# Selective attention and a low-rank mixer on one core: the first two batches are fed in another order

## The chip, the cores and the metric

One core of a Trainium2 chip runs the whole kernel as one program. The metric is device time in microseconds; the median of three runs before the change is 416.16 (416.15 to 417.01).

The engines: TensorE (PE; PEld is its weight load), VectorE (DVE), ScalarE (ACT), GpSimd (POOL) and SyncE (SP). Each runs its own instructions in order. "SPq", "ACTq" and "POOLq" are those engines' queues in which they issue DMAs; a DMA that waits there holds all that is behind it.

## The reference, cut to what matters

Eight batches, eight heads, 576 positions, head size 64. Attention with a causal mask and a bias from running sums of a gate s, then a mixer over 576 positions of width 512.

```python
scores = (q @ k.T) / sqrt(D)
cum    = cumsum(maximum(s, 0))
scores = where(causal, -1e9, scores + minimum(-(cum[:, None] - cum[None, :]), 0))
x      = softmax(scores) @ v            # heads side by side: 576 x 512
u = x + (x.T @ U @ V).T                 # rank 32
out = u + maximum(u @ w_ch1, 0) @ w_ch2 # 512 -> 2048 -> 512
```

Inputs and output are float32; the kernel computes in bfloat16 with float32 sums.

## The kernel before, in words

**Tiling.** The batches go in four groups of two (`GROUPS`). A group has 1152 rows, nine tiles of 128; tile 4 (`TAIL`) holds the last 64 rows of both batches. For a group: attention of both batches fills `x_sb`, `mix` (batch 0 alone: `mix_first`) turns it into `uT`, `layer1` gives `hT` and `layer2` the output, which goes out by SP (L508, L513).

**Scores.** q and k lie in `qT` and `kT` with the head size on the partitions, two heads (a pair n) to a buffer, in a ring of eight. Four more partitions, D to KA, hold the bias as products: rows of `parts` (a running sum split into bfloat16 pieces, and its negative) against rows of ones. So a score with its bias is one matmul over 68 rows (L280). `scores` computes a head in four PSUM banks, ACT takes the exponential of each (L286), POOL zeroes the upper triangle of five diagonal blocks (L299), and `weigh` multiplies by v (L326) and normalises on DVE (L332, L334, L339). Batch 0 has eight probability tiles of its own (`first_p`), three of them lent from `x_sb[1]` and `v_raw[1]`; later heads rotate over five.

**How q and k come in.** For batches 0 and 1: `load_six` (POOL's queue, with a cast) into a corner of `hT`, then `turn_six`: six PE transposes (L260) and two copies (L272). Batch 1 does its eight turns inside `attention(1)`, two ahead of head 0 and one in each of heads 0 to 5. For batches 2 to 7: `cast(b)` (L144, POOL's queue) writes bfloat16 copies to DRAM (`kq_rows`), and `turn_kq(n)` (L163, SP's queue) reads a pair back with a transposing DMA; `bias_rows(n)` (L251, SP) then overwrites partitions D to KA from `aug_rows` in DRAM, so it waits for that pair's transposes. The 64 elements behind each pair in `kq_rows` are zeros that the transposed read runs into.

**The sums.** `cumulate(b0, b1)` is a generator in steps: gate and scans (L212, L214), a small matmul that adds the sums of earlier segments (L217), then additions and splits into `parts` (L219 to L226), all on DVE. For batches 0 and 1 `direct_rows` (L231) writes `parts` straight into `qA` and `kA`. For batches 2 to 7 `later_sums` runs `cumulate(2, B)`, clears `ones` and `zeros` on POOL, sends them to `aug_rows` and `kq_rows` (L633, L634), and `keep_rows` (L238) sends `parts` to `aug_rows`. It is called after batch 1 and ahead of the turned loads of batch 2; its tiles are lent from `x_sb[1]`.

**v.** `fetch_v(b, t)` (L176) brings a tile as float32 into `vf`; `cast_v` (L182, POOL) copies it into `v_raw`. One `vf` serves all batches, so a batch's loads wait for the casts of the one before. Batch 0 is fetched on ACT's queue at the very start.

**Order around the change.** It is written out by hand (`manual_schedule`). `first_attention` is batch 0: three turns, then scores of eight heads with the other turns in between; two heads are weighed after head 6, six at the end, with `mix_first` in two halves. `beside(back, ahead, ratio, lead)` interleaves two generators by their estimated PE time: `layer1` of batch 0 beside `attention(1)` and `mix(0)`, then the layers of group g beside the attention of group g + 1. `at_head(h)` hangs work on other queues on a head: weight loads, casts of q and k, casts of v. SP's order after batch 1 is:

```python
    for n in range(8, 16):
        if n == 12:
            for t in range(5):
                fetch_v(3, t)
        turn_kq(n)
        if n > 8:
            bias_rows(n - 1)
```

From batch 2 on, every second head queues `bias_rows(n + 7)` and `turn_kq(n + 8)`, and head 7 of batch c the loads of v of batch c + 2. The casts of v of batch c + 1 stand in POOL's queue at heads 5 to 7 of batch c, ahead of the next head's mask.

The lines are those of the kernel before:

Of the kernel before, what the change touches and what calls it, by code (L numbers as in the profile page):

```python
# [40 lines left out]
def kernel(  # L41
# [34 lines left out]
    v_raw = [const([128, 10, H, D + 1], BF16, f"v_raw{i}") for i in range(2)]  # L76
# [23 lines left out]
    def clear(ap, value=0.0, engine=None):  # L100
# [11 lines left out]
    lent = x_sb[1].rearrange("p t c -> p (t c)")  # L112
    run_all, cum_all = (
        lent[: SEG * H, many * i : many * i + many].bitcast(FP32) for i in range(2)
    )
    ones, zeros = lent[:BH, 2 * many : 2 * many + S], lent[:BH, 2 * many + S : 2 * many + S + D]
# [25 lines left out]
    def cast(b):  # L142
        for i, src in enumerate((k, q)):
            nc.gpsimd.dma_start(  # L144
                out=kq[i, HP * b : HP * b + HP, :PAIR].rearrange("n (r c) -> r n c", r=128),
                in_=src[b]
                .rearrange("(n h) s d -> n (h s d)", h=2)
                .rearrange("n (r c) -> r n c", r=128),
            )
# [53 lines left out]
    def cumulate(b0, b1):  # L203
# [19 lines left out]
        nc.vector.tensor_sub(rest, cum, pt[:, 1])  # L223
        nc.vector.tensor_copy(pt[:, 2], rest)
        yield
        nc.vector.tensor_sub(pt[:, 3], rest, pt[:, 2])  # L226
# [49 lines left out]
    def scores(n, hh, p):  # L276
# [11 lines left out]
        ps = bank("s", 3)  # L288
        one(ps, 0, S - 128, 512, 64)
# [14 lines left out]
        ps = bank("s", 3)  # L304
        one(ps, 0, 0, 128, 448)
# [38 lines left out]
    spare = v_raw[1].rearrange("p t h e -> p (t h e)")  # L344
    first_p = pT + [lent[:, :P_W], lent[:, P_W : 2 * P_W], spare[:, :P_W]]
# [187 lines left out]
    for t in (4, 0, 1, 2, 3):  # L533
        fetch_v(0, t, nc.scalar)
    load_six(0, 0, 0, 2)
    nc.vector.memset(before, 1.0)
    nc.vector.memset(warm, 0.0)
    nc.scalar.activation(warm, warm, EXP)
    before_v = before.rearrange("p (h j) -> p h j", j=SEG)
# [8 lines left out]
    load_six(0, 1, 0, 2)  # L548
# [4 lines left out]

    for t in (kT[0], qT[0]):
        clear(t[D:KA, : 2 * S], 1.0)
    sums = cumulate(0, 2)
# [3 lines left out]
    for i in range(2, HP):  # L560
        for t in (kT[i], qT[i]):
            clear(t[D:KA, : 2 * S], 1.0, nc.gpsimd)
    next(sums)
# [7 lines left out]
    for r in range(AUG):  # L571
        direct_rows(0, 1, HP, r)
    load_UV()
    load_s(2, B)

    for p in first_p:
        nc.gpsimd.memset(p[:, PAD:D4], 1.0)

    def first_attention():
        turn_six(0, 0, 0)  # L580
        turn_six(0, 0, 1, scalar=2)
# [3 lines left out]
        for h in range(H):  # L585
            p = next_p()
            quanta = scores(h // 2, h % 2, p)
# [13 lines left out]
            if h == 2:  # L601
                cast_v(0, 4)
                load_w1(0)
                load_w1(1)
                cast_v(0, 2)
                cast_v(0, 3)
                cast_v(0, 0, nc.vector)
                cast_v(0, 1, nc.vector)
            if h == 3:
                place_UV(0)  # L610
                for t in range(5):
                    fetch_v(1, t)
            if 3 < h < 6:
                clear((kA, qA)[h - 4][1][D:KA], 1.0, nc.gpsimd)
# [11 lines left out]
        for _ in mix_first(2):  # L626
            pass

    def later_sums():
        yield from cumulate(2, B)  # L630
        clear(ones, 1.0, nc.gpsimd)
        clear(zeros, 0.0, nc.gpsimd)
# [123 lines left out]
```

## Time and profile before

| what | value |
|---|---|
| median of 3 runs | 416.16 us |
| profiled execution, its time | 419.31 us |
| its span | 417.5 us |
| PE busy | 377.2 us, 90% |
| PEld, DVE, ACT, POOL busy | 235.8, 146.3, 202.1, 105.2 us |
| share of the chain that ended last | PE 81%, DVE 5%, DMA 4%, POOL 3% |
| DMA: SP's queue (q1), POOL's (q0), ACT's (q10) | 38.4%, 20.7%, 1.5% of 16 engines' span |
| moved | 48.55 MB, mean 116 GB/s |

The profile is of one execution. "busy" is the time in which an engine ran an instruction; "idle before, releaser" is the time an instruction's engine stood still and what ended it. In rows of the order of time, the first number is the start and the second the length of a merged run of instructions, both in us; a row of a queue covers the issue and not the transfer. PEclk is the granted share of TensorE's clock. A DMA share over 1 means that transfers overlap on an engine.

### The profile page before, as it was taken

The numbers are of one execution on the slowest core, as the hardware profiler recorded it, in microseconds if no ns is written. First come the engines' busy times: TensorE is split into PE (matmuls) and PEld (weight loads), VectorE is DVE, ScalarE is ACT, GpSimd is POOL, SyncE is SP. The second block draws the span as 40 slices with busy tenths as digits, with TensorE's granted clock in tenths as the row PEclk, the third lists the DMA queues.
The fourth block names the chain that finished last, engine by engine and source line by source line (L and its number), as shares of the span: only waits on it lengthen the run. The fifth ranks groups of instructions, "written<-read, shape, count | busy, mean of one in ns | idle before, by whom it ended". The sixth has DMA issues, their size and how long they took to land.

```text
span 417.5 us, 8214 instructions
## 1 busy us (share of the span) xinstructions
PE 377.2 (90%) x3255; PEld 235.8 (56%) x3278; DVE 146.3 (35%) x317; ACT 202.1 (48%) x472; POOL 105.2 (25%) x170
## 2 busy tenths in 40 slices
PE   2698799999689819999999999999999999999996
PEld 1576686547467514566665545666665455665442
DVE  6657584812113304811113348111123373000221
ACT  2581486308658600098896400688875002775000
POOL 7498267003234121032332300123222000000000
PEclk9999699999969968999999999999999999999999
DMA  9599999499989896998896991100001111000121
GB/s 164 100 169 178 194 183 202 91 155 172 203 152 215 145 173 122 200 201 184 176 189 106 192 215 52 54 0 2 2 2 52 51 52 75 2 0 2 75 77 75
DMA packets 117943, 48.55 MB, mean 116 GB/s; under 512 B 99536, under 2 KB 113040, under 8 KB 117904
## 3 DMA queue, kind: packets, MB, share of 16 engines
q1 hardware_dynamic: 99424, 33.21, 38.4%
q0 software_dynamic: 13792, 13.63, 20.7%
q10 hardware_dynamic: 4688, 1.18, 1.5%
q8 instruction: 26, 0.43, 0.4%
q14 instruction: 13, 0.11, 0.1%
HBM read 37.52 MB, written 16.97 MB: 131 GB/s over the span
## 4 chain that ended last, share of the span: by engine, by line
PE 81%; DVE 5%; DMA 4%; POOL 3%; ACT 2%; issue 2%; SPq 1%; ACTq 0%; POOLq 0%; DVEq 0%
PE ps_f L481 29%; PE ps_f L496 28%; PE ps_s L280 10%; PE ps_pv L326 8%; PE ps_f L423 2%; PE ps_pv L441 2%; PE ps_f L456 1%; ACT pT L286 1%; SPq L163 1%; DMA kT<-parts 1%; POOL pT L299 1%; ACT hT L488 1%; DVE x_sb L460 1%; DMA qT<-kq_rows 1%; DMA vf<-in_v_dram 1%
## 5 line engine op out<-in xcount | busy, mean ns | idle before, releaser
L481 PE MATMUL ps_f<-uT,w 128*128 128x384 bf16 (+1 forms) x832 | 161.2, 318 | 0.3 <-ACT hT L488 0.3
L286 ACT ACTIVATE pT<-ps_s 128x448 bf16<-128x448 f32 x244 | 115.4, 517 | 91.9 <-PE ps_s L280 90.5
L496 PE MATMUL ps_f<-w,hT 128*128 128x512 bf16 x554 | 139.9, 381 | 1.4 <-issue 0.2
L488 ACT ACTIVATE hT<-ps_f 128x384 bf16<-128x384 f32 (+1 forms) x208 | 99.1, 477 | 71.8 <-PE ps_f L481 70.5
L280 PE MATMUL ps_s<-qT,kT 68*128 68x128 bf16 (+4 forms) x576 | 87.1, 258 | 13.0 <-DMA qT<-aug_rows 5.7
L299 POOL TENSOR_SCALAR_AFFINE_SELECT pT<-pT 128x640 bf16<-128x640 bf16 x61 | 45.8, 751 | 200.8 <-ACT pT L286 200.5
L481 PEld LDWEIGHTS <-w 128*128 128x128 bf16 x832 | 74.1, 99 | 34.9 <-issue 1.5
L496 PEld LDWEIGHTS <-hT 128*128 128x128 bf16 x576 | 53.3, 98 | 55.3 <-issue 2.7
L280 PEld LDWEIGHTS <-kT 68*128 68x128 bf16 x576 | 49.9, 104 | 43.2 <-issue 15.9
L332 DVE RECIPROCAL rec<-ps_pv 128x5 f32<-128x5 f32 x64 | 12.5, 195 | 146.9 <-PE ps_pv L326 146.4
L505 DVE TENSOR_TENSOR o<-x_sb,ps_f 128x512 f32<-128x512 bf16 x36 | 24.7, 686 | 91.6 <-PE ps_f L496 81.5
L326 PE MATMUL ps_pv<-v_raw,pT 128*128 128x65 bf16 x915 | 41.9, 201 | 10.7 <-POOL pT L299 9.6
L326 PEld LDWEIGHTS <-pT 128*128 128x128 bf16 x915 | 38.6, 102 | 19.4 <-POOL pT L299 10.4
L334 DVE TENSOR_TENSOR x_sb<-ps_pv,rec 128x320 bf16<-128x320 f32 (+1 forms) x64 | 29.3, 458 | 2.5 <-ACT pT L286 0.4
L182 POOL CAST v_raw<-vf 128x512 bf16<-128x512 f32 (+1 forms) x38 | 22.9, 618 | 14.6 <-DMA vf<-in_v_dram 14.0
L460 DVE TENSOR_TENSOR x_sb<-x_sb,ps_f 128x512 bf16<-128x512 bf16 x32 | 21.2, 686 | 5.3 <-PE ps_f L456 5.1
L448 DVE COPY uT<-ps_pv 128x1024 bf16<-128x1024 bf16 (+2 forms) x18 | 11.1, 624 | 2.6 <-PE ps_pv L441 2.4
L272 DVE COPY kT<-ps_pv 64x576 bf16<-64x576 bf16 x12 | 9.6, 799 | 4.3 <-PE ps_pv L260 4.2
L441 PEld LDWEIGHTS <-x_sb 128*128 128x128 bf16 x128 | 8.7, 98 | 3.8
L456 PE MATMUL ps_f<-ux_sb,V_cat 128*128 128x512 bf16 x27 | 10.2, 379 | 0.6 <-DVE o L505 0.4
L260 PEld LDWEIGHTS <-hT 96*128 96x128 bf16 x96 | 7.3, 125 | 5.2 <-DMA hT<-in_q_dram 2.7
L441 PE MATMUL ps_pv<-identity,x_sb 128*128 128x128 bf16 x128 | 10.2, 219 | 0.0
(88 smaller groups left out, 131.8 us busy)
## 6 DMA issues: line engine op xcount, KB each, us to landing
out_dram<-o SPq DMA_DIRECT2D x32, 256.0 KB
vf<-in_v_dram SPq DMA_DIRECT2D x28, 256.0 KB
w<-in_moe_w_ch_dram POOLq DMA_DIRECT2D x8, 512.0 KB, 8.7
kq_rows<-in_k_dram POOLq DMA_DIRECT2D x6, 576.0 KB, 7.9
kq_rows<-in_q_dram POOLq DMA_DIRECT2D x6, 576.0 KB, 10.5
vf<-in_v_dram ACTq DMA_DIRECT2D x4, 256.0 KB
out_dram<-o SPq DMA_DIRECT2D x8, 128.0 KB
vf<-in_v_dram SPq DMA_DIRECT2D x7, 128.0 KB
```

Source lines behind the costliest of these rows:

```text
L182: (engine or nc.gpsimd).tensor_copy(v_raw[b // 2 % 2][n, 5 * (b % 2) + t, :, :D], vf[n, t])
L280: nc.tensor.matmul(ps[:, col : col + w], lhsT=kt_[:KA, c + kc : c + kc + 128], rhs=qt_[:KA, c + qc : c + qc + w], start=True, stop=True,)
L286: nc.scalar.activation(p[:, at : at + w], ps[:, :w], EXP, scale=scale)
L299: nc.gpsimd.affine_select(out=diagonal, in_=diagonal, compare_op=ALU.is_ge, fill=0.0, base=0, pattern=[[0, 5], [1, 128]], channel_multipli ...
L326: nc.tensor.matmul(pv3[:, it, :], lhsT=p[:, at : at + 128], rhs=vr[:, 5 * bi + j, h, :], start=(j == 0), stop=(j == it),)
L334: nc.vector.tensor_mul(x[:, 5 * bi : 5 * bi + n, h * D : h * D + D], pv3[:, :n, :D], rec[:, :n].unsqueeze(2).to_broadcast([128, n, D]),)
L441: nc.tensor.transpose(pb[:, d, m, :], x[:, t, 128 * d : 128 * d + 128], identity)
L460: nc.vector.tensor_add(x[:, t, :], x[:, t, :], hp_)
L481: nc.tensor.matmul(f1[:, :cw], lhsT=w1[:, kt, 128 * nf : 128 * nf + 128], rhs=uT[:, kt, c0:c1], start=(kt == 0), stop=(kt == 3),)
L488: nc.scalar.activation(hT[:, nf, c0:c1], f1[:, :cw], RELU)
L496: nc.tensor.matmul(f2, lhsT=hT[:, kt, 128 * t : 128 * t + 128], rhs=w2[:, kt, :], start=(kt == 0), stop=(kt == 15 and not more),)
L505: nc.vector.tensor_add(o, x_sb[g % 2][:, t, :], f2)
```

## The change

- The tiles of the later sums, `ones` and `zeros` are lent from `v_raw[1]` instead of `x_sb[1]`. `ones` and `zeros` are cleared and sent in head 2 of batch 0. `cumulate(2, B)` is taken apart: scans in head 3 of batch 0 (DVE), the small matmul, its addition (DVE) and a copy and a product (now POOL) in head 4, two more steps on POOL in heads 0 and 1 of batch 1, `keep_rows` in head 3 of batch 1. `later_sums` is gone.
- v of batch 0 is fetched on SP's queue behind the bias rows of batch 0, not on ACT's at the start; its casts are all on POOL in head 3 (two were on DVE). s of the later batches comes ahead of U and V.
- The rows of ones of batch 1 come from `aug_rows` by two DMAs; two POOL clears of `kA[1]` and `qA[1]` are gone. The bias rows of batch 1 and the first half of its q and k are queued in `first_attention`.
- The first two turns of batch 1 move into the second half of `mix_first`; the other six follow two heads earlier.
- `cast` writes runs of 2304 elements instead of 576.
- Products of zeros on PE (`fill`): five of 512 columns before the first sums, six before the third turn, two of 384 in each head of batch 0. The matrix is the first tile of `x_sb[0]`, and the scores overwrite what they write.
- The second load of batch 0 is issued ahead of two masks on POOL; `scalar=2` (copies on ACT) moves from the second turn to the first; the place of `place_UV` shifts by one head.

```diff
-    lent = x_sb[1].rearrange("p t c -> p (t c)")
+    lent = [x_sb[1].rearrange("p t c -> p (t c)"), v_flat[1]]
...
-                out=kq[i, HP * b : HP * b + HP, :PAIR].rearrange("n (r c) -> r n c", r=128),
+                out=kq[i, HP * b : HP * b + HP, :PAIR].rearrange("n (r c) -> r n c", r=32),
...
-    def cumulate(b0, b1):
+    def cumulate(b0, b1, engine=nc.vector):
...
+        nc.vector.tensor_add(cum, run, ps[:n, :nb].unsqueeze(2).to_broadcast([n, nb, CW]))
         yield
-        nc.vector.tensor_add(cum, run, ps[:n, :nb].unsqueeze(2).to_broadcast([n, nb, CW]))
-        nc.vector.tensor_copy(pt[:, 1], cum)
-        nc.vector.tensor_scalar_mul(pt[:, 0], pt[:, 1], -1.0)
+        engine.tensor_copy(pt[:, 1], cum)
+        engine.tensor_scalar_mul(pt[:, 0], pt[:, 1], -1.0)
...
+    def fill(ps, w):
+        nc.tensor.matmul(ps[:, :w], lhsT=zero[:, :128], rhs=zero[:, :w], start=True, stop=True)
...
-        turns = [(hp, which) for hp in range(HP) for which in range(2)] if b == 1 else []
+        turns = [(hp, which) for hp in range(HP) for which in range(2)][2:] if b == 1 else []
...
-    for t in (4, 0, 1, 2, 3):
-        fetch_v(0, t, nc.scalar)
...
+    zero = x_sb[0][:, 0, :]
+    clear(zero)
...
+    for t in (4, 0, 1, 2, 3):
+        fetch_v(0, t)
+    load_s(2, B)
     load_UV()
-    load_s(2, B)
+    later = cumulate(2, B, nc.gpsimd)
...
-            quanta = scores(h // 2, h % 2, p)
+            quanta = scores(h // 2, h % 2, p, fills=384)
...
             if h == 2:
+                clear(ones, 1.0, nc.gpsimd)
+                clear(zeros, 0.0, nc.gpsimd)
+                nc.sync.dma_start(out=kq[:, :, PAIR:].rearrange("i n c -> (i n) c"), in_=zeros)
+                nc.sync.dma_start(
+                    out=aug[1:4].rearrange("r n s -> n r s"),
+                    in_=ones.unsqueeze(1).to_broadcast([BH, 3, S]),
+                )
+            if h == 3:
                 cast_v(0, 4)
                 load_w1(0)
                 load_w1(1)
...
+                next(later)
+            if h == 4:
+                place_UV(0)
+                next(later)
+                next(later)
             done.append((0, h, p))
             if h == 6:
+                load_six(1, 0, 0, 4)
+                load_six(1, 1, 0, 4)
...
+        nc.sync.dma_start(out=kA[1][D : D + 1], in_=aug_v[3:4, HP : 2 * HP])
+        nc.sync.dma_start(out=qA[1][D + 1 : KA], in_=aug_v[1:4, HP : 2 * HP])
+        for r in range(AUG):
+            direct_rows(1, 0, HP, r)
...
-        for _ in mix_first(2):
+        half = mix_first(2)
+        next(half)
+        turn_six(1, 0, 0)
+        turn_six(1, 0, 1)
+        for _ in half:
             pass
-    def later_sums():
...
     def at_head(h):
-        if h == 2:
+        if h < 2:
+            next(later)
+        if h == 3:
             place_UV(1)
+            keep_rows(2, B)
...
-    for _ in later_sums():
-        pass
```

More of the change, by code (lines that the diff above doesn't have):

```diff
@@ L111 @@
     many = 2 * (B - 2) * CW
[L112 removed]
+    lent = [x_sb[1].rearrange("p t c -> p (t c)"), v_flat[1]]
     run_all, cum_all = (
[L114 to L116 removed]
+        lent[1][: SEG * H, P_W + many * i : P_W + many * i + many].bitcast(FP32)
+        for i in range(2)
+    )
+    at = P_W + 2 * many
+    ones, zeros = lent[1][:BH, at : at + S], lent[1][:BH, at + S : at + S + D]
     U_f = stage[:, : 5 * R].rearrange("p (t r) -> p t r", r=R)
@@ L555 @@
         clear(t[D:KA, : 2 * S], 1.0)
+    ps = bank("s", 3)
+    for _ in range(5):
+        fill(ps, 512)
     sums = cumulate(0, 2)
```

67 lines of the change are left out of this document (27 added, 40 removed).

## The prediction

> **What bounds the kernel now.** I read the slices of the page first, then the stages around the weak slices, then the order of time of TensorE, of SyncE's queue and of GpSimd in those stages, then the DMA issues. Slices of 10.4 us:
>
> ```profile
> PE   2698799999689819999999999999999999999996
> ...
> PEclk9999699999969968999999999999999999999999
> DMA  9599999499989896998896991100001111000121
> ```
>
> TensorE (PE) is full from slice 15 to the end. It is weak at the start, in slice 10, and in slices 13 and 14, and after each of those holes its granted clock is low too. The DMA engines are busy for the first 250 us, with one hole in slice 7. The stages (columns: PE, PEld, DVE, ACT, POOL busy, clock, DMA share, GB/s):
>
> ```profile
> 110.00:118.00 8.00, 2.28 (x17) 1.59 (x15) 0.19 (x1) 2.17 (x7) 1.22 (x2) 0.83 0.96 189
> ...
> 140.00:154.00 14.00, 5.13 (x53) 2.92 (x50) 1.82 (x6) 3.80 (x9) 1.52 (x3) 0.84 0.72 147
> 154.00:176.00 22.00, 20.45 (x135) 10.93 (x138) 13.12 (x24) 0.93 (x2) 3.64 (x6) 0.87 0.84 160
> 176.00:264.00 88.00, 87.28 (x775) 53.17 (x780) 28.96 (x65) 48.44 (x112) 20.49 (x30) 1.00 0.84 163
> ```
>
> From 176 on PE has nothing to lose. The two holes, in the order of time of PE and of GpSimd (POOL):
>
> ```profile
> 116.44 0.53 PE L280 MATMUL ps_s<-qT,kT 68*128 68x64 bf16 x4 [5.72 <-DMA qT<-aug_rows]
> ...
> 154.59 1.01 PE L326 MATMUL ps_pv<-v_raw,pT 128*128 128x65 bf16 x15 [9.41 <-POOL pT L299]
> ...
> 153.23 0.61 POOL L182 CAST v_raw<-vf 128x512 bf16<-128x512 f32 x1 [12.18 <-DMA vf<-in_v_dram]
> ```
>
> The first hole waits for the bias rows of the last head pair of batch 2. In the second, POOL sits in a cast of v of batch 4 whose load has not landed, and the masking behind it holds PE. Both loads stand in SyncE's (SP's) queue, which runs in order:
>
> ```profile
> 71.59 0.56 SPq L633 DMA_DIRECT2D kq_rows<-x_sb  x1
> ...
> 81.56 1.84 SPq L238 DMA_DIRECT2D aug_rows<-parts  x4
> 83.58 1.32 SPq L163 DMA_TRANSPOSE kT<-kq_rows  x1
> 84.99 1.53 SPq L163 DMA_TRANSPOSE qT<-kq_rows  x1
> ...
> 98.55 11.32 SPq L176 DMA_DIRECT2D vf<-in_v_dram  x5
> ...
> 113.77 0.28 SPq L251 DMA_DIRECT2D qT<-aug_rows  x1
> ...
> 149.74 4.20 SPq L176 DMA_DIRECT2D vf<-in_v_dram  x5
> ```
>
> The queue stands still until 71.59 behind POOL's two clears (`ones`, `zeros`), then until 81.56 for the sums on DVE, and only then begins the turned loads of batch 2. From 83.58 to 149.74 it is late all the way. So the time is set by when SP begins at L163, plus 66.2 us of its own work to the load of v of batch 4, plus what PE has left after 154.59. That is the number to move.
>
> **The later sums, ones rows and zeros (the part that decides).** All that the queue waited for at 71.59 and 81.56 goes away: ones and zeros are written in head 2 of batch 0, the scans go in head 3, the rest on POOL by head 1 of batch 1, and the four `keep_rows` are queued in head 3 (before: about 56 us). What ends last for the first turned load is then the cast of k of batch 2 into DRAM. In the DMA issues it is sent at 59.97 and takes 9.4 us: 69.4. The q cast, sent at 60.71, takes 13.2: 73.9. The casts of batch 3 land at 76.1 and 79.7 (62.88 + 13.2, 63.60 + 16.1). So SP's start moves from 83.58 to somewhere between 69.4 (14.2 us gained) and 79.7 (3.9, if the transposes get nothing beside the casts). I take the second transfer, 84.99 to 73.9, as the step that holds the rest in order: 11.1.
>
> Then the contention. Five v loads take 7.74 us (24.31) and 7.86 (36.79) where they share little, and 11.32 at 98.55 beside the two casts of batch 4: a pair of casts costs the queue about 3.5 us. In the new order the first transposes stand beside the casts of batch 3 (3.5 lost), the v loads come ahead of the casts of batch 4 (3.5 won back), and the transposes after them take those casts instead (3.5 lost): 11.1 - 3.5 = 7.6 by that count, 11.1 if transposes, which SP issues only every 1.3 to 1.5 us, lose less than v loads do. I take 10 and keep 7.6 to 11.1.
>
> The first hole closes within this: bias rows land at 116.3 - 10 = 106.3 and PE stands for them from 110.7. That gives 5.72, and the slow stretch behind it: granted clock 0.67 in 114 to 118 and 0.50 in 118 to 122, so about 2.7 of the time to 121.8. The PE that comes 8.4 us earlier then meets the second hole sooner: it would stop at 145.2 - 8.4 = 136.8 and go on at 154.6 - 10 = 144.6. The second hole stays, at 7.8 us, with its slow stretch. This is where the gain ends, and why it is 10 and not the 20 of both holes.
>
> **POOL's new work.** Copy, multiply, subtract, copy, subtract over 72x384, four of them beside or between the masks of 0.75 us. On DVE they took 0.36, 0.22, 0.55, 0.36 and 0.56. POOL's nearest rows are casts of 0.62 for 128x512. Bounds: 2.0 us (as on DVE) to 4 (twice). In batch 1 the masks come every 3 us with 2 us idle ahead of them (2.28, 2.39), so 0.9 to 1.8 in head 0 beside a weight load's issue of 0.77 just fits: 0, and at worst 0.5 once. Two clears of 2.01 leave POOL and two casts of 0.6 come to it from DVE: it is lighter.
>
> The Trainium skill (GPSIMD Engine Reference, Elementwise side by side) has a two-input operation about 1.96 times slower on GpSimd than on VectorE. No run here shows it; by it the two subtractions would be about 1.1 us each, an estimate, inside those bounds.
>
> **v of batch 0 on SP behind the rows.** Five issues leave ScalarE's queue (5.37 us) and five come to SP, ahead of s and U, V. Before, the first scores waited for rows sent at 8.05 that landed at 13.39, 5.3 us, while v held 45% of the DMA engines in 0 to 7 us and 41% in 7 to 14. A small transfer on idle engines took 1.85 (s, at 0.81). First scores at 10.2 to 13.4; I take 11: 2.5 won. v then is sent from about 12 to 18 and lands by about 20; POOL wants it in head 3, near 20. Cover: the scores of three heads. If gone, POOL's weight loads, v of batch 1 and everything behind wait for it.
>
> **Products of zeros.** Cold, 512 columns take 0.43 (the pairs of L496 in 155 to 157 are 0.85), warm 0.22. Eleven of 512 and sixteen of 384 are 9.9 us cold, 5 warm. The eleven lie in PE's idle time before the first scores (11.3 us idle of 14). The sixteen lie beside the exponentials, which take 1.7 us a head while PE has 1.4 cold and 0.7 warm for the scores; two products more are 0.64 or 0.32. The first three heads also have transposes and run 2.5 us a head, bound by PE. So the products cost up to 3 x 0.64 + 5 x 0.3 = 3.4 if PE stays cold, and win up to 3 x 0.8 = 2.4 if it is warm; later weighs then run at 0.46 instead of 0.83. Two new waits of PE lie here: its matmul of the later sums in head 4 waits for DVE's scans (1.6 us, queued behind the last copy of turns), about 1.5; and the products of head 7 read `x_sb`, which DVE has just written: rec and product, 0.7. What is queued behind each is the next head's scores, and ScalarE waits for them.
>
> **Turns ahead.** Four copies of 0.8 us move ahead of the uT copies: layer 1 begins up to 3.2 later, but the scores no longer wait 2.82 for them (43.99). Even. Then the second half of q and k of batch 1 is wanted in head 0 instead of head 2, near 45; it lands at 39.14 + 9.5 = 48.6. A stall of up to 3.6 if the start came early, 0 otherwise.
>
> Together the start lies between 6 us earlier and 4 later, and none of it reaches the end: PE has 7.8 us of waiting left at the second hole, and the casts queue behind weight loads that keep the DMA engines full from 64 to 70 (share 121.8%, 208 GB/s). I count 0.
>
> **Longer runs in casts.** That same row bounds it: one queue alone already fills the engines. 0; at best, a tenth of four casts' 2.8 us of transfer each, 1 us. The Trainium skill (DMA: Bandwidth & Descriptors, Specifications) asks 512 B for line rate, and both forms are above it: it also gives 0.
>
> **Sum.** The profiled execution took 419.31 with a span of 417.5; the median is 416.16. 417.5 - 10 = 407.5 of span, and against the median 416.2 - 10 = 406.
>
> **Rivals.**
> 1. The second hole goes too. For: between 141 and 149 the DMA share is low, so the queue there waits link by link (transpose landed, then bias, then the next), and if it comes before the casts of batch 5 instead of beside them the links shorten. PE then loses neither hole: 5.7 + 2.7 + 9.4 + 2.5 (cold to 159.6) + 0.6 at 78 to 80 = 20.9, time 395. Against: it needs 18 us, more than 14.2. Chance 0.20.
> 2. Casts starve the transposes. In 100 to 102 the cast queue had 108.6% of the engines and SP's queue 0.0%, with one packet. Then the start is 79.7, 3.9 gained: 412. Chance 0.15. By the Trainium skill (DMA: Bandwidth & Descriptors, Queues, rings and completion order) an engine takes turns between queues packet by packet, a packet being many descriptors; longer runs would make the casts' turns longer, and that row agrees.
> 3. Slower: v of batch 0 lands so late that POOL stands in its cast in head 3, with both weight loads, v of batch 1, the halves of q and k and the casts of batch 2 behind it. It turns slower where the casts come over 14.2 us late, v landing after 34. For: SP's v loads have taken 11.3 us and three transfers are behind it. Against: two such stretches end at 12 + 11.3 + 3.4 = 27. At 38 it would be 4 slower, 420. Chance 0.06.
> 4. It changes nothing at the end, because some other wait in front of 83.58 (a lane of earlier transfers) keeps SP: 416. Chance 0.03.
>
> **How the numbers follow.** Forecast 0.54 (gain 7 to 13, 403 to 409), rivals 0.20, 0.15, 0.06, 0.03, and 0.02 for more than rival 1. Likeliest: 406. The range reaches to both neighbours, 394 to 412, and leaves out rivals 3 and 4, the last, and the outer part of rival 1: under 0.2. Faster by over 0.2% (0.8 us, what a measurement here can tell): 0.54 + 0.20 + 0.15 + 0.02, less 0.01 for a weak rival 2: 0.90. Within: 0.03 and that 0.01; slower 0.06.
>
> **What would show it.** Right: L163 begins at 70 to 75 on SP; no wait of PE for aug_rows near 105; a POOL wait for vf of about 8 us near 137, ended near 143; PE over 95% behind it. Wrong: L163 at 79 or later; the wait for vf gone or over 11 us; a POOL wait for vf near 20; PE slow through batch 0.

## The result and the profile after

| kernel | median (range, runs) | span of the profiled execution | mean granted clock |
|---|---|---|---|
| before | 416.96 us (415.37 to 419.43, 20) | 417.5 us | 0.969 |
| changed | 419.07 us (417.28 to 422.52, 20) | 420.7 us | 0.943 |

The ratio is 1.006, with a 95% interval of 1.0038 to 1.0083. The change makes the kernel slightly slower, where 406 was forecast. Ratios leave out runs that fell in a slower state (two of e7's six), so for e7 the ratio is to be read and not the median.

Each profile is of one execution, and the two compared here lie above their medians: 419.31 us for the kernel before, and 422.52, the longest of the 20, for the changed one. Points of time in them vary by some us from one execution to another: e12 below is the kernel before up to batch 2, and in its profile the casts of batch 2 are sent 3.4 us earlier than in the profile of the kernel before (56.55 and 59.97).

The new kernel's lines are numbered a little higher: the turned loads L163 are L166, the loads of v L176 are L179, the casts of v L182 are L185, the bias rows L251 are L254, the scores L280 are L287. The slices of the changed kernel's page:

```profile
PE   6798479899999709999999999999999999999996
...
PEclk9556969999999958999999999999999999999999
DMA  7979899999999989799697793100001111000121
```

The dip of slice 10 is gone. A dip in slices 4 and 5 is new, and the hole in slices 13 and 14 is now a 7 and a 0. The stages, in the same columns as before:

```profile
110.00:118.00 8.00, 8.00 (x109) 6.40 (x108) 1.97 (x7) 7.76 (x22) 2.15 (x3) 1.00 0.99 184
140.00:154.00 14.00, 4.93 (x46) 2.78 (x45) 1.82 (x6) 3.63 (x8) 0.75 (x1) 0.79 0.77 106
154.00:176.00 22.00, 16.56 (x110) 8.67 (x113) 10.44 (x20) 0.93 (x2) 4.42 (x7) 0.82 0.89 159
176.00:264.00 88.00, 87.28 (x781) 53.40 (x785) 30.95 (x69) 48.43 (x112) 19.79 (x30) 1.00 0.85 170
```

TensorE (PE) works through 110 to 118, where it had 2.28 us of work before, and loses more in 140 to 176. From 176 on both kernels are alike. The waits of PE, then those of GpSimd (POOL), in order of time:

```profile
13.10 0.91 PE L287 MATMUL ps_s<-qT,kT 68*128 68x64 bf16 x6 [4.19 <-DMA kT<-parts]
55.06 0.66 PE L263 MATMUL ps_pv<-identity,hT 96*128 96x96 bf16 x6 [6.18 <-DMA hT<-in_k_dram]
158.48 1.01 PE L337 MATMUL ps_pv<-v_raw,pT 128*128 128x65 bf16 x15 [13.50 <-POOL pT L308]
```

```profile
42.95 2.97 POOL L185 CAST v_raw<-vf 64x512 bf16<-64x512 f32 x5 [7.62 <-DMA vf<-in_v_dram]
45.86 0.77 POOL L188 DMA_DIRECT2D w<-in_moe_w_ch_dram  x1
46.62 0.68 POOL L156 DMA_DIRECT2D hT<-in_k_dram  x1
...
69.68 0.57 POOL L147 DMA_DIRECT2D kq_rows<-in_k_dram  x1
70.25 0.56 POOL L147 DMA_DIRECT2D kq_rows<-in_q_dram  x1
...
157.12 0.61 POOL L185 CAST v_raw<-vf 128x512 bf16<-128x512 f32 x1 [16.27 <-DMA vf<-in_v_dram]
```

The same instructions of POOL before:

```profile
35.48 2.96 POOL L182 CAST v_raw<-vf 64x512 bf16<-64x512 f32 x5 [0.95 <-DMA vf<-in_v_dram]
...
39.14 0.68 POOL L153 DMA_DIRECT2D hT<-in_k_dram  x1
...
59.97 0.75 POOL L144 DMA_DIRECT2D kq_rows<-in_k_dram  x1
```

SP's queue after:

```profile
26.70 8.27 SPq L179 DMA_DIRECT2D vf<-in_v_dram  x5
...
48.56 12.60 SPq L241 DMA_DIRECT2D aug_rows<-parts  x4
77.48 3.37 SPq L166 DMA_TRANSPOSE kT<-kq_rows  x1
80.95 5.20 SPq L166 DMA_TRANSPOSE qT<-kq_rows  x1
...
107.48 3.95 SPq L166 DMA_TRANSPOSE kT<-kq_rows  x1
111.53 3.82 SPq L166 DMA_TRANSPOSE qT<-kq_rows  x1
...
127.97 1.24 SPq L166 DMA_TRANSPOSE kT<-kq_rows  x1
129.31 10.05 SPq L166 DMA_TRANSPOSE qT<-kq_rows  x1
...
153.55 4.36 SPq L179 DMA_DIRECT2D vf<-in_v_dram  x5
```

Read from the end. The load of v of batch 4 is issued at 153.55 instead of 149.74, 3.8 us later. The span is 3.2 longer. Span less the issue of this load is 267.8 before and 267.2 after; in e1 to e9 below it lies between 267.0 and 268.2. So the time is still set by that load, as the prediction said, and the question is why it came late although SP began its turned loads 6.1 us earlier (83.58 to 77.48). By this rule and the medians, the load of a usual execution would stand at about 147.7 before and 149.8 after (an estimate: median, less 1.8 between time and span, less 267.5).

**The start moved by less than forecast.** `keep_rows` is indeed over early (its row starts at 48.56 and takes 12.60). But the casts of batch 2 are sent at 69.68, not at 59.97 as before, and land 7.6 us later, at 77.3: what SP then waits for. They are late because POOL sends them at head 4 of batch 1, and batch 1 is late. PE stands 6.18 us before 55.06 for the second half of k of batch 1, which POOL sent at 46.62 (39.14 before), because it stood 7.62 in the cast of v of batch 1 (42.95; before at 35.48, after a wait of 0.95).

All of batch 1 moves with this: PE begins the scores of batch 2 at 103.43 instead of 95.22.

**The way from there to the load grew.** It was 66.2 us before (83.58 to 149.74) and is 76.1 now. The rows of SP's queue on this way, added up by kind (us, rounded):

| | before | changed | e5 (below) |
|---|---|---|---|
| 22 turned loads (turns 8 to 18, k and q) | 36.6 | 51.8 | 47.9 |
| v of batch 3 | 11.3 | 4.1 | 4.2 |
| bias rows and stores | 9.0 | 8.8 | 9.1 |
| between the rows | 9.2 | 11.4 | 10.7 |
| the whole way | 66.2 | 76.1 | 71.8 |

So the turned loads take the time. The long ones stand beside casts that are landing: turn 8 (77.48 and 80.95) beside those of batch 3, sent at 71.50 and 72.04; turn 13 (107.48 and 111.53) beside those of batch 4, sent at 105.74 and 106.28; turn 16 (129.31, 10.05 us) beside those of batch 5, sent at 128.30 and 128.84. Before, the casts of batch 3 had landed when SP began, those of batch 4 met the loads of v of batch 3 (11.32 us), and only turn 16 met casts (6.33 at 130.65). Turn 13 was short then:

```profile
114.14 1.21 SPq L163 DMA_TRANSPOSE kT<-kq_rows  x1
115.40 1.32 SPq L163 DMA_TRANSPOSE qT<-kq_rows  x1
```

In the eleven profiles with this order of the queue (before, changed, e1 to e9), every part of a turned load on this way that took over 3.5 us began within 14 us of the sending of casts.

The view of waits names other engines for this time. After, in 95 to 156 (total, times, longest, us):

```profile
SPq L166 <- PE ps_f L491: 4.7, 2, 3.8
SPq L166 <- DVE rec L343: 4.6, 2, 3.7
```

That reading does not hold. L491 is a matmul of layer 1 and L343 a reciprocal, and neither touches q or k. A turned load overwrites a buffer of the ring of eight; turn 13 takes one of batch 1, whose last scores are over by 77. The two longest of these waits are the rows of turn 13 themselves. A releaser in a view of waits is inferred, and here it is only what happened to end last.

### The profile page after: what moved, and what is told of

It is laid out like the page before. It is cut to its first block, busy times and chain, and to the rows that moved or that the text cites. A ratio compares the mean times of both kernels' runs of the same rounds, so it can differ in the third digit from the quotient of the medians.

```text
span 420.7 us, 8268 instructions
## 1 busy us (share of the span) xinstructions
PE 382.5 (91%) x3282; PEld 237.2 (56%) x3305; DVE 143.4 (34%) x311; ACT 202.2 (48%) x472; POOL 103.8 (25%) x175
## 4 chain that ended last, share of the span: by engine, by line
PE 77%; issue 6%; DMA 5%; POOL 5%; DVE 3%; ACT 3%; SPq 0%; POOLq 0%; ACTq 0%; DVEq 0%
PE ps_f L491 28%; PE ps_f L506 27%; PE ps_s L287 9%; PE ps_pv L337 6%; DMA vf<-in_v_dram 2%; ACT pT L293 2%; DMA hT<-in_k_dram 2%; PE ps_f L433 2%; PE ps_pv L451 2%; PE ps_f L466 1%; POOL v_raw L185 1%; POOL pT L308 1%; DMA kT<-parts 1%; ACT hT L498 1%; DVE x_sb L470 1%
## 5 line engine op out<-in xcount | busy, mean ns | idle before, releaser
L491 PE MATMUL ps_f<-uT,w 128*128 128x384 bf16 (+1 forms) x832 | 158.7, 315 | 1.2 <-ACT uT L423 0.5
L491 PEld LDWEIGHTS <-w 128*128 128x128 bf16 x832 | 73.3, 98 | 35.9 <-issue 2.8
L287 PE MATMUL ps_s<-qT,kT 68*128 68x128 bf16 (+4 forms) x576 | 86.7, 256 | 4.5 <-DMA kT<-parts 4.2
L287 PEld LDWEIGHTS <-kT 68*128 68x128 bf16 x576 | 50.3, 103 | 34.2 <-issue 10.1
L343 DVE RECIPROCAL rec<-ps_pv 128x5 f32<-128x5 f32 x64 | 12.5, 195 | 148.6 <-PE ps_pv L337 148.2
L337 PE MATMUL ps_pv<-v_raw,pT 128*128 128x65 bf16 x915 | 41.0, 199 | 15.0 <-POOL pT L308 13.7
L337 PEld LDWEIGHTS <-pT 128*128 128x128 bf16 x915 | 37.7, 101 | 24.0 <-POOL pT L308 14.9
L185 POOL CAST v_raw<-vf 128x512 bf16<-128x512 f32 (+1 forms) x40 | 23.9, 617 | 25.3 <-DMA vf<-in_v_dram 24.7
L281 PE MATMUL ps_s<-x_sb 128*128 128x384 bf16 (+1 forms) x27 | 12.9, 544 | 2.2 <-DVE x_sb L103 1.4
L263 PE MATMUL ps_pv<-identity,hT 96*128 96x96 bf16 x72 | 6.4, 242 | 7.3 <-DMA hT<-in_k_dram 6.9
L458 DVE COPY uT<-ps_pv 128x1024 bf16<-128x1024 bf16 (+2 forms) x18 | 11.1, 624 | 2.6 <-PE ps_pv L451 2.4
```

The source lines that it names most:

```text
L185: (engine or nc.gpsimd).tensor_copy(v_raw[b // 2 % 2][n, 5 * (b % 2) + t, :, :D], vf[n, t])
L287: nc.tensor.matmul(ps[:, col : col + w], lhsT=kt_[:KA, c + kc : c + kc + 128], rhs=qt_[:KA, c + qc : c + qc + w], start=True, stop=True,)
L337: nc.tensor.matmul(pv3[:, it, :], lhsT=p[:, at : at + 128], rhs=vr[:, 5 * bi + j, h, :], start=(j == 0), stop=(j == it),)
L491: nc.tensor.matmul(f1[:, :cw], lhsT=w1[:, kt, 128 * nf : 128 * nf + 128], rhs=uT[:, kt, c0:c1], start=(kt == 0), stop=(kt == 3),)
```

## The experiments

### Parts of the change undone (e1 to e4)

Each starts from the changed kernel: runs of 576 elements in the casts again (e1), no products of zeros (e2), all eight turns of batch 1 back in `attention(1)` (e3), all three together (e4).

```diff
-                ...rearrange("n (r c) -> r n c", r=32),     # e1, e4
+                ...rearrange("n (r c) -> r n c", r=128),
-            quanta = scores(h // 2, h % 2, p, fills=384)    # e2, e4 (and the eleven fills of 512)
+            quanta = scores(h // 2, h % 2, p)
-        turns = [...][2:] if b == 1 else []                 # e3, e4 (and the two in mix_first)
+        turns = [...] if b == 1 else []
```

> The changed kernel with the casts' runs back at 576 elements (r=128). Theory A (long runs in the casts of batch 5 and the transposed loads of turn 16 slow each other: in the changed kernel the two casts sent at 128.3 and 128.8 take 12.1 and 15.7 us to land, before 8.4 and 10.4, and the bias rows behind turn 16 go at 144.35 instead of 140.11): the casts of batch 5 land in 8 to 10.5 us, the load of v of batch 4 goes about 4 us earlier (149.5), the wait of POOL for it falls from 16.3 to about 12, time about 415 (4 less than the changed kernel). Theory B (the queue is only late from batch 1 on, runs do nothing): casts and time as in the changed kernel, 419.

Measured 419.47 us (418.4 to 421.5), ratio 1.0066 (1.004 to 1.0092): the time of the changed kernel (419.07). With the shorter runs turn 16 did not stand 10 us, and turn 16 to the load of v took 20.1 us instead of 25.6, but the time is the same, and so is the sum of the turned loads of e2, which keeps the long runs (45.9 and 46.2 us). Turn 16's q part took 3.84 in e2, so the 10 us seem to belong to the one execution of 422.52 us that was profiled; they are not what makes the change slow.

> The changed kernel without the products of zeros and their zero tile. Theory A (in batch 0 PE stays at the half clock all the time and the sixteen products of 384, 0.31 us each, lie on its path): the scores of head 7 end about 4 to 5 us earlier (from 34.4 to about 30), all that follows on POOL's queue comes 2 to 4 earlier, time 2 to 4 less (415 to 417). Theory B (the exponentials and v of batch 1 hide them): head 7 up to 1 us earlier, time the same within 0.5. Theory C (they warm the clock): PE slower without them, granted clock in 26 to 40 lower, time 1 to 3 more.

Measured 418.02 (416.3 to 419.63), ratio 1.0028 (1.0001 to 1.0055): 1.1 less by the medians, which is within the noise (the intervals of this ratio and of the changed kernel's overlap), though the matmul that closes the first half of `mix_first` came 3.4 earlier (36.21 instead of 39.61). What was won there was waited for again: 5.91 for the same load of k of batch 1.

> The changed kernel with all eight turns of batch 1 back in its attention (two ahead of head 0, then heads 0 to 5). Theory A (the turn that was moved ahead waits 6.2 us for the second half of k, lands at 55.0, and the casts of batches 2 and 3 hang on the heads behind it): no wait of PE on hT at 49 to 55, a wait of about 3 for the copies instead, casts sent about 3 to 5 us earlier (65 to 67 instead of 69.7), first turned load as much earlier, time 2 to 4 less. Theory B (what counts is only the meeting of casts and turned loads at 130 to 144): the casts are earlier, the load of v of batch 4 is not, time the same within 1.

Measured 415.45 (412.7 to 418.49), ratio 0.9965 (0.9926 to 1.0004): 3.6 won. PE's 6.18 are gone:

```profile
46.72 0.36 PE L287 MATMUL ps_s<-qT,kT 68*128 68x64 bf16 x4 [2.83 <-DVE qT L275]
55.36 0.43 PE L263 MATMUL ps_pv<-identity,hT 96*128 96x96 bf16 x6 [1.30 <-DMA hT<-in_k_dram]
```

The casts of batch 2 go out at 63.29 instead of 69.68, and the load of v of batch 4 is issued at 146.21 instead of 153.55. So the turns ahead, which ask for the second half of q and k two heads earlier, are the largest loss of these three. The same wait can be taken away from its other end (e7).

> The changed kernel with short runs, without products of zeros, with the turns back: what is left are the early sums and ones rows, v of batch 0 on SyncE's queue and the early first half of q and k. If the three losses add up (about 4, 2 to 4, 2 to 4): 408 to 411, the first turned load at about 74 instead of 80.9, the load of v of batch 4 at 141 to 144. If they are one loss told three times (only the latest wait counts): 415. If the early sums have no worth of their own: 416 to 417, as before the change.

Measured 414.43 (413.07 to 417.02), ratio 0.994 (0.9909 to 0.9971): 4.6 won in all, near the sum of the three as measured and far from the 408 to 411 expected if three larger losses added up. The load of v of batch 4 is issued at 145.39, not at 141 to 144.

### The early sums alone, and what feeds batch 1 (e5 to e8)

e5 is the kernel before with only the later sums, `ones`, `zeros` and `keep_rows` early, on POOL as in the change. e6 is e4 with v of batch 0 back on ScalarE's queue at the start; e7 is the changed kernel with that alone. e8 is e4 with three loads in front of the casts of v of batch 1 in POOL's queue:

```diff
+    load_w1(2)
+    load_six(1, 0, 4, 8)
+    load_six(1, 1, 4, 8)
     for t in (4, 0, 1, 2, 3):
         cast_v(1, t)
-    load_w1(2)
-    load_six(1, 0, 4, 8)
-    load_six(1, 1, 4, 8)
     load_w1(3)
```

The edit of e5 against the kernel before, cut to where the steps go:

```diff
+    later = cumulate(2, B, nc.gpsimd)        # tiles lent from v_raw[1]
...
             if h == 2:                       # batch 0
+                clear(ones, 1.0, nc.gpsimd)
+                clear(zeros, 0.0, nc.gpsimd)
+                ...                          # both sent on SP
...
+                next(later)                  # h == 3; twice more at h == 4
...
     def at_head(h):                          # batch 1
+        if h < 2:
+            next(later)
+        if h == 3:
+            keep_rows(2, B)
...
-    for _ in later_sums():
-        pass
```

and that of e6 and e7:

```diff
+    for t in (4, 0, 1, 2, 3):
+        fetch_v(0, t, nc.scalar)             # ahead of the second loads of q and k
...
-    for t in (4, 0, 1, 2, 3):
-        fetch_v(0, t)
...
-            if h == 3:
                 cast_v(0, 4)                 # at head 2 again, with the two weight loads
...
-                for t in range(4):
-                    cast_v(0, t)
+                cast_v(0, 2)
+                cast_v(0, 3)
+                cast_v(0, 0, nc.vector)
+                cast_v(0, 1, nc.vector)
```

> The kernel before with one part of the change alone: later sums in steps (scans in head 3 of batch 0, POOL in head 4 and in heads 0 and 1 of batch 1, rows kept in head 3), ones and zeros in head 2, tiles lent from v_raw[1]. Theory A (this part is worth what was forecast, and the rest of the change loses it by making v of batch 1, and all POOL sends behind its casts, 7 us late): casts of batch 2 sent at about 60, first turned load at 69 to 75 instead of 83.6, load of v of batch 4 at 139 to 143 instead of 149.7, time 406 to 410. Theory B (the load of v of batch 4 is held by the meeting with the casts of batch 5 and the chain of links behind it, not by the queue's start): first turned load early, load of v of batch 4 at 146 or later, time 413 to 417; only the hole at 111 to 116 goes and comes back in the second one.

Measured 412.51 (411.07 to 413.91), ratio 0.9891 (0.9863 to 0.9919). The early sums are worth 4.4 us alone, less than the forecast's 10; load and time lie between the two theories, nearer to B. The first turned load starts at 73.11 (inside the forecast's 70 to 75), 10.5 earlier than before, yet the load of v of batch 4 comes only 4.8 earlier, at 144.94. The rest is lost on the way, which is 71.8 us long instead of 66.2: SP now meets the casts of batch 3 with turn 8 and those of batch 4 with turn 13 (6.89 us for its q part).

> The changed kernel with short runs, no products of zeros, turns back, and also v of batch 0 back on ScalarE's queue at the start with its casts and the weight loads in head 2. Left of the change: early sums, ones rows by DMA, first half of q and k of batch 1 sent after head 6. Against e4 it moves v of batch 0 alone. Theory A (the later casts of v of batch 0 put the two weight loads, sent at 23.4 to 24.9 instead of 21.1, and v of batch 1 on the DMA engines together; v of batch 1 then lands at 42 instead of 35.5): v of batch 1 cast at 35 to 37, second weight load and halves of q and k sent 5 to 7 earlier than in e4, time 406 to 410, 4 to 8 under e4. Theory B: it lands at 42 whatever starts it, since the first half of q and k comes in its way; time as e4, 414.

Measured 414.05 (411.83 to 416.99), ratio 0.9939 (0.9914 to 0.9963): no gain over e4. Theory B holds: v of batch 1 still lands at 41.

> The changed kernel with v of batch 0 back on ScalarE's queue, casts and weight loads in head 2; long runs, products of zeros and turns ahead stay. Theory A: v of batch 1 lands at about 36 to 38, the stall of 6.2 at 49 to 55 for the second half of k shrinks to 0 to 2, casts sent 5 to 8 earlier, time 408 to 413. Theory B: the stall and the time stay, 418 to 420.

Measured 414.33 (409.69 to 418.98, 6 runs), ratio 0.9882 (0.9831 to 0.9933). PE has no wait over 0.9 left in batch 1, and the casts of batch 2 leave at 65.84. By the ratios (1.006 and 0.9882) this is some 7 us less than the changed kernel, theory A; the intervals allow 5 to 10. POOL comes to the cast of v of batch 1 at 37.36 and does not wait there, so the second half of k is sent at 41.03 instead of 46.62. So PE's wait for it needs two parts of the change together, the turns ahead and v of batch 0 behind the rows; undoing either one removes it or most of it. Why v of batch 1 lands early here and only at 41 in e6 is open.

> e4 with POOL's third weight load and the second halves of q and k of batch 1 sent ahead of the casts of v of batch 1 (only the fourth weight load stays behind). Theory A (those loads are late because POOL stands 7.9 us in front of them, in the cast of v of batch 1): the half of k lands before 47, no wait of PE at 55 (3.2 in e4), casts 3 to 6 earlier, time 409 to 412, if v of batch 1 lands by 48. Theory B (the DMA engines are full, so what is sent first makes v of batch 1 late by as much): POOL waits for v to 47 to 50, the mask of head 0 of batch 1 and PE behind it, time 414 to 418.

Measured 411.2 (410.54 to 412.28), ratio 0.9864 (0.9839 to 0.9889): 3.2 less than e4, as theory A has it. The casts of batch 2 leave at 60.57 and the first turned load starts at 69.95. POOL's wait for v of batch 4 is 12.29 all the same:

```profile
144.29 0.61 POOL L185 CAST v_raw<-vf 128x512 bf16<-128x512 f32 x1 [12.29 <-DMA vf<-in_v_dram]
```

Between the kernel before and e8 SP's start has moved by 13.6 us, the load of v by 8.9, the time by some 6.

### The second hole itself (e9 to e12)

In all these kernels turn 16 is followed by the load of v of batch 4 about 20 us later (18.9 to 20.9; 25.6 in the changed kernel's profile). Two explanations were left: the casts of batch 5, which turn 16 meets, or the load's place behind turns 16 to 18. e9 is e8 with these casts four heads later:

```diff
-            if h == 0 and c + 2 < B:
+            if h == (4 if c == 3 else 0) and c + 2 < B:
                 cast(c + 2)
```

(with the turned loads of batch 5 held back to head 5). e10 is e8 with the queue's order changed; e11 is the changed kernel and e12 the kernel before with the same edit:

```diff
             if h % 2 and b >= 2:
-                bias_rows(n + RING - 1)
-                turn_kq(n + RING)
+                if h == 1:
+                    bias_rows(n + RING - 1)
+                if h == 7 or b > 2:      # batch 2: turns 16 to 18 wait for head 7, behind fetch_v(4)
+                    for m in range(HP * b, n + 1) if b == 2 else (n,):
+                        if m % HP:
+                            bias_rows(m + RING - 1)
+                        turn_kq(m + RING)
```

> The kernel of e8 with one thing changed: the two casts of batch 5 are sent at head 4 of batch 3 instead of head 0, and the turned loads of batch 5 (20 to 22) follow at head 5. So turn 16 no longer meets these casts. Theory A, the meeting makes the 19.5 us between the issue of turn 16 (121.35 in e8) and the load of v of batch 4 (140.81): turn 16's q part stood 5.65 us and landed at about 131; without the casts it lands as later turns do, about 3 us after issue, so the load comes about 5 us earlier, near 136, GpSimd's wait for it falls from 12.3 to about 7.5, and the time from 411.2 to about 406. Theory B, the queue goes link by link whatever shares it: the load stays within 1 us of 140.8 and the time within 1 us of 411.2.

Measured 409.87 (409.35 to 413.18), ratio 0.9857 (0.9812 to 0.9902): the same as e8's 0.9864. The load is issued at 140.26, 18.9 after turn 16, as by theory B. The test is not clean: the casts, sent at 130.23, now meet turn 18, whose q part took 4.90, while turn 16's q part took 1.43 instead of 5.65 in e8. So the long row goes where the casts go, which is the plainest sign that they make it long, and taking them away from turn 16 alone won nothing.

> The kernel of e8 with v of batch 4 loaded ahead of the turned loads 16 to 18 in SyncE's queue; these and their bias rows follow behind it, at head 7 of batch 2. Theory A, the second hole is nothing but this load's place in the queue: it is issued as soon as the last cast of v of batch 3 has freed its tile (116.7 in e8), at about 118, GpSimd's wait of 12.3 for it is gone, TensorE loses neither the 9.5 of its wait nor about 2.5 of cold clock behind it: 411.2 - 12 = about 399, and the rule that the span is 267 to 268 behind this load's issue ends here. Theory B, the whole queue is late: the turned loads and bias rows of batch 4, about 5 us later than in e8, are then what TensorE waits for at the start of batch 4, and at most 4 us are won: 407 or more.

Measured 399.78 (399.01 to 400.33), ratio 0.9597 (0.9556 to 0.9638). Theory A, within 1 us. The load on SP, POOL's cast of v of batch 4 and the stage of the hole in e10:

```profile
120.39 8.61 SPq L179 DMA_DIRECT2D vf<-in_v_dram  x5
```

```profile
133.24 0.61 POOL L185 CAST v_raw<-vf 128x512 bf16<-128x512 f32 x1
```

```profile
140.00:154.00 14.00, 13.42 (x79) 6.54 (x78) 9.59 (x17) 0.00 (x0) 0.00 (x0) 1.00 0.71 128
```

The load is issued 20 us earlier than in e8. The cast has no wait beside it any more, and PE is busy 13.42 of 14 us at full granted clock, where e8 has 8.24 at 0.58. The queue's turns 16 to 18 come later and nobody waits for them: PE has no wait of 0.9 us or more behind 47 in its merged rows. Span less issue is now 277.6: the rule ends.

> The changed kernel as it is, with v of batch 4 loaded ahead of the turned loads 16 to 18 as in e10. Theory A: TensorE's wait of 13.5 and some 2.5 of cold clock go: 419 - 16 = about 403. Theory B: the turned loads become the wait, 4 us at most are won: 415 or more.

Measured 408.47 (408.06 to 410.07), ratio 0.9818 (0.978 to 0.9856): the hole is gone, and 10.6 are won of the 16 expected, between the two theories. The 13.5 in that sum came from that execution of 422.52 us; in those of e1 and e2 the same wait is 8.38 and 7.86.

> The kernel before with v of batch 4 loaded ahead of the turned loads 16 to 18 as in e10, and nothing of the change. Theory A: TensorE's wait of 9.4 and some 2.5 of cold clock go, the first hole (5.7 and its cold clock) stays: 417 - 12 = about 405; so with that hole gone the change would be worth about 2 us (403 in e11), its gain in the first hole less what it loses in batches 0 and 1. Theory B: at most 4 us are won, 413 or more.

Measured 405.77 (403.14 to 407.18), ratio 0.9733 (0.9688 to 0.9778). Theory A. One reordering of SP's queue wins 11 us in the kernel before, and with it the changed kernel is the slower one by 2.7. So the second hole hid from the end not only gains of the change but losses too.

### What the change itself is worth (e13 to e16)

All have v of batch 4 first: the changed kernel with the turns back (e13), without the products of zeros (e14), with both undone (e16), and the kernel before with the early sums alone, as e5 (e15). The edits are those shown above.

> The kernel of e11 (changed, v of batch 4 first) with the turns of batch 1 back in attention(1), as in e3. Theory A, what the change loses in batches 0 and 1 shows in full once the second hole is gone: the 6.57 of TensorE's wait for the second half of k at 55.8 and about 2 of cold clock behind it go, some 2 to 3 of it come back as waits near 46, as in e3 (2.83 and 1.30): 408.5 - 5 = about 403. Theory B, another wait takes its place: 407 or more.

Measured 403.12 (401.94 to 405.29), ratio 0.9685 (0.9644 to 0.9727): theory A. The wait that e11 has, and the two that e13 has in its place:

```profile
55.80 0.66 PE L263 MATMUL ps_pv<-identity,hT 96*128 96x96 bf16 x6 [6.57 <-DMA hT<-in_k_dram]
```

```profile
46.83 0.36 PE L287 MATMUL ps_s<-qT,kT 68*128 68x64 bf16 x4 [2.83 <-DVE qT L275]
55.42 0.43 PE L263 MATMUL ps_pv<-identity,hT 96*128 96x96 bf16 x6 [1.25 <-DMA hT<-in_k_dram]
```

> The kernel of e11 without the products of zeros, as in e2. In e2 the matmul that closes the first half of mix_first came at 36.21 instead of 39.61, 3.4 earlier, but batch 1 then waited 5.91 for its q and k. Theory A: TensorE is early and waits for the same load, since that load's time is set by GpSimd's queue: within 1 us of 408.5. Theory B: the 3.4 stay: about 405.

Measured 407.5 (405.94 to 408.76), ratio 0.9783 (0.9742 to 0.9824): 1.0 less than e11, as by theory A. PE is earlier and waits for the same load, 7.75 us instead of 6.57.

> The kernel before with the early later sums, ones rows and zeros (as e5) and with v of batch 4 loaded first (as e12), nothing else of the change. Theory A, the early sums close the first hole (5.26 and about 2.7 of cold clock in e12) and cost the wait of 4.3 for the scans in batch 0: 405.8 - 8 + 4 = about 402. Theory B, the first hole closes only to open another wait: 405 or more.

Measured 401.7 (401.02 to 405.05), ratio 0.9659 (0.9613 to 0.9705): theory A. The first hole is closed, no wait of PE over 0.6 us is left behind 49, and PE waits 4.37 us in batch 0 for the scans on VectorE (DVE), the cost that was expected for it.

> The kernel of e11 with both undone, the products of zeros and the turns ahead; it differs from e10 by the longer runs and by the order of the loads in front of the casts of v of batch 1. If those two edits are all that the change loses, about 401 to 402 (408.5 less 3.4 and less 4 to 5), near e10's 399.8; if what they lose overlaps (one wait of batch 1 for q and k), about 403 to 405.

Measured 402.04 (400.22 to 402.84), ratio 0.9649 (0.9604 to 0.9693): near the expected 401 to 402. What is left to e10's 399.8, the loads ahead of the casts of v of batch 1 and the shorter runs, is within the noise.

With the hole out of the way the parts show at their own size (differences of medians): early sums -4.1 (e12 to e15), turns ahead +5.4 (e13 to e11), products of zeros +1.0 and +1.1 (e14 to e11, e16 to e13), the loads ahead and the shorter runs together -2.3 (e16 to e10). The intervals of the ratios are about 2 us wide to each side, so the first two are clear of noise and the others are not.

## Why the prediction was wrong

- **What bounds the kernel.** Right. The time hangs on the load of v of batch 4, and behind it nothing is lost: span less its issue stayed within 267.0 to 268.2 in eleven profiles, and moving the load ended it.
- **"SP's start moves ... the second transfer, 84.99 to 73.9".** The first failed step. The casts of batch 2 were taken as sent at 59.97, as before. They are hung on head 4 of batch 1, so what batches 0 and 1 lose reaches them. They left at 69.68, and the two transfers moved from 83.58 and 84.99 to 77.48 and 80.95: 6.1 and 4.0 us instead of 11.1.
- **"Together the start lies between 6 us earlier and 4 later, and none of it reaches the end".** The term behind that step, mis-sized and then counted 0. PE begins batch 2 8.2 us later. The turns ahead were given a stall of up to 3.6 and made 6.18 (e3: 3.6 of time), since the half of k was sent 7.5 us later than the 39.14 of the sum; the products of zeros were given up to 3.4 and made 3.4 at `mix_first` (e2: some 1 us of time, within the noise). With the shorter runs they cost 4.6 together (e4). "PE has 7.8 us of waiting left at the second hole" hides a delay only on the way through PE; here it went through POOL's queue into SP's, which had no slack.
- **The contention, "11.1 - 3.5 = 7.6 by that count ... I take 10".** The second failed step, also a matter of size. Where a way of 66.2 us was to grow by 1.1, or 3.5 at worst, it grew by 9.9 in the changed profile and by 3.7 to 5.7 in e1 to e9. In the changed profile the meeting with the casts of batch 3 cost 5.7 (turn 8: 8.57 us instead of 2.85) and that with the casts of batch 4 cost 5.2 (turn 13: 7.77 instead of 2.53), where 3.5 was taken for each; the loads of v won back 7.2, not 3.5; and turn 16 beside the casts of batch 5, counted as unchanged, cost 3.6 more. In e5, where the start did move by 10.5, the load moved by 4.8. The forecast's mechanism alone was worth 4.4 us, not 10.
- **The first hole** closed as forecast, with its cold stretch (PE 8.00 of 8.00 in 110 to 118). In the changed kernel this is partly luck: PE comes to it 8.2 us later, which alone is more than the 5.72 of that wait. e15 shows that the early sums close it by themselves.
- **The second hole** was forecast at 7.8 us for PE, from 136.8 on. PE stops at 145.0, as before (145.2): what the first hole gave was lost in batches 0 and 1. The wait is 13.50 in the profile of 422.52 us, 8.38 and 7.86 in e1 and e2. That these two agree with the forecast is luck, since both ends of the wait came 8 to 10 us later than forecast.
- **POOL's steps** took 0.50, 1.18, 0.90, 0.50 and 0.91: 4.0 us, the upper bound. One subtraction takes 0.90 instead of 0.55 on DVE, 1.6 times. The Trainium skill (GPSIMD Engine Reference, Elementwise side by side) has 1.96 for a larger float32 addition; at this size the measured factor is lower.
- **v of batch 0 behind the rows.** First scores at 13.10, not 11: the rows that they wait for are still 4.19 late, so v had not held them by more than the 0.5 us that was won. e6 and e7 say that its place costs nothing where the turns are back and some 7 us where they are ahead.
- **Longer runs in casts:** 0, as forecast (e1).
- **The rivals.** Rival 1's end, about 395 with both holes gone, was real (e10 takes 399.8) but not reached by an earlier start. Rival 3 came nearest: the chain it names (w1, v of batch 1, the halves of q and k, the casts of batch 2) is the one that ran late, by 9.7 us. It was held harmless below 14.2, since it was weighed against the whole gain of the start and not against what SP would lose later. Rival 2's mechanism is there too, in part: SP's first turned loads met the casts of batch 3 and took 3.37 and 5.20 us, but they were not held until those had landed (83.2 and 86.3). That longer runs lengthen such meetings does not show (e1 and e2).

Still open is how much of the 5 to 6 us from one turn to the next (e9: 121.41, 127.45, 132.72) is transfer and how much is the bias rows' wait for it; e9 took the casts from turn 16 but not from turn 18.

## What to carry to other kernels

The time between two points of an in-order queue is not its "own work". Before moving its start, ask what each of its transfers will then stand beside, and price every such meeting from a row that shows one; here the transfers that came earlier met casts that they had missed before. Do not take the engine that a view of waits names as the cause until its instruction is seen to read or write the same tile. When a part ahead is made later, ask for every queue which instructions are hung on that part, and follow the delay through them; slack on the busiest engine covers only its own path. And where one late load ends a hole, try its place in the queue first: here that single reordering won 11 us (e12), more than any part of the change, and with it the rest could be judged.

## What the runs showed of the hardware

PE's matmuls in batch 0 stay slow through long busy stretches, with products of zeros between them or without. The 448-column scores in 14 to 36 (columns: busy us, mean ns, idle before), first in the kernel before, then in the changed one:

```profile
L280 PE MATMUL ps_s<-qT,kT 68*128 68x448 bf16 x8 | 4.6, 577 | 0.0
```

```profile
L287 PE MATMUL ps_s<-qT,kT 68*128 68x448 bf16 x8 | 4.6, 578 | 0.0
```

In 180 to 260 the same form takes 354 in both. PE was busy for 20.96 and 20.75 of the 22 us, and the zeros changed the duration by nothing. The clock column does not show this: at these equal durations it reads 1.00 in the stretch before and 0.50 after. So there the durations are to be read and not the column. The Trainium skill (TensorE: Matmul & The Clock Gate, Part 1) has full rate after about 3.4 us of sustained work; in 14 to 20 of the changed kernel PE was busy 6.00 of 6.00 us and in 26 to 30 4.00 of 4.00, and the mean over the whole 22 us stays at the slow duration. There the measurement decides: these stretches did not bring full rate. (A busy PE is modelled, so short stops inside such a stretch would not show.)

Parts of turned loads in SP's queue take mostly 1.2 to 1.7 us, and 3 to 10 us beside casts of another queue that are landing (turn 13: 1.21 and 1.32 us away from them, 3.95 and 3.82 beside them). What makes them long inside the DMA is not shown.
